# An attention and routing kernel: two pools change places, fills move ahead of a small load, token rows grow from 2052 to 2112 bytes

## Chip, core and metric

The kernel runs on one core of a Trainium2 chip. Its time is device time in microseconds of one execution; three runs of the kernel before gave 434.67, 436.81 and 437.12, median 436.81. Engines are called TensorE (PE in the rows, its weight loads PEld), VectorE (DVE), ScalarE (ACT), GpSimd (POOL) and SyncE (SP). DMA transfers are issued by SyncE's queue (SPq) and by GpSimd (POOLq) and run on the core's 16 DMA engines.

## What is computed

Attention over chunks of 32 positions, then a mixture of experts in which every token goes to exactly one of eight experts. Each expert takes at most 384 tokens, and the pairs of token and expert are served in order of their logits.

```python
for c in range(nc):                       # 24 chunks of 32, for 4 x 8 heads of 64
    k_full = np.concatenate([mem_k, k_ctx], axis=2)      # 8 memory keys, 16 left, 32, 8 right
    scores = scale * np.matmul(q_c, k_full.transpose(0, 1, 3, 2))
    a = np.exp(scores - max); a = a / (sum + 1e-09)
    out[:, :, c_start:c_end] = np.matmul(a, v_full)
x = out.transpose(0, 2, 1, 3).reshape(3072, 512)
logits = x @ w_gate                       # 3072 x 8
for idx in np.argsort(-logits.flatten()): # greedy, an expert full at 384 tokens
    ...
for e in range(8):
    out[mask] = np.maximum(x[mask] @ w1[e], 0.0) @ w2[e] # 512 -> 1024 -> 512
```

## The kernel before

**Attention.** The 3072 tokens are 24 tiles of 128. `attention` runs them as a software pipeline written out by hand: `plan` lists its steps (scores, softmax, transposes, product with the values, norm, rows, logits) with the number of tiles by which each lags. Keys and values come in through five buffers `kvb` in the pool `kvbuf`, which are filled with zeros once at the start by VectorE, ScalarE and GpSimd. Right after these fills GpSimd makes the identity matrix for the transposes (L75, L76). All other tiles of the attention are in the pool `abuf`.

**Token rows.** `rows` writes each attention row as a pair of half-precision parts into the tile `keep` (L173, L174), 24 rows of `XW` elements a partition. `release` adds the scale of the row, one 32-bit number in the last two elements (L181), and writes the 128 rows of a tile to the DRAM tensor `xs` (L182). Tiles 0 to 20 are released late, when the last keys and values have been asked for: ten of them in one go by `rest`, near 107 us. The last two, 22 and 23, wait for the last norms, between the steps of the first routing. One such transfer is 128 pieces of `XW` elements.

**Routing.** `phase` finds the tokens of an expert by a histogram search on VectorE and TensorE and ends in a number of an expert, `ei` (L551). Small transposes of an identity on TensorE (`fill`, L466) fill its idle time in the first phase. `tokens` makes the list `ids` (L653) and gathers the expert's 384 rows from `xs` into three tiles `xg` by indirect DMA from GpSimd (L658). For the first expert three things stand ahead of the gathers on GpSimd: `farr`, an indirect gather of 128 times the same row of the constants, that nothing reads; `seen`, a load of four bytes from each 128th row of `xs`, that nothing reads either, but that makes GpSimd wait for all writes of `xs`; and fills of one partition of each `xg`.

**Experts.** `loads` brings the weights `w1f`, `w2f` from SyncE, four transfers of half a megabyte for each matrix, at an address that SyncE loads from `ei` (L748, L751). `weights` takes the largest value (L770 on ScalarE; for the first expert half of the last part on VectorE, L773), makes a power of two of it, and rounds the weights to a high part (ScalarE) and a low one (GpSimd). `turn` transposes the first expert's rows on TensorE (L688); later ones are transposed by DMA (L670). `gemm` multiplies: L902 and L912 into `ps_hid`, L929 into `ps_y`. `output` scales the result by the number that came along in the row (L878) and `scatter` writes it out.

**What sets the order.** From the routing on, `Lines` merges these generators by costs and due times when the kernel is built; each engine then runs its instructions in that order, and the framework adds the semaphore waits. Pools are stacks of tiles in the on-chip memory. `abuf` was opened first and `kvbuf` after it; both close when the attention is done, and `wbuf`, which holds `xg`, the weights and all else of the experts, begins at the place where the first of them began. A transfer into `wbuf` therefore waits for those that used that place.

Of the kernel before, what the change touches and what calls it, by code (L numbers as in the profile page):

```python
# [11 lines left out]
F32 = mybir.dt.float32  # L12
F16 = mybir.dt.float16
BF16 = mybir.dt.bfloat16
I32 = mybir.dt.int32
AF = mybir.ActivationFunctionType
ALU = mybir.AluOpType
AX = mybir.AxisListType

P = 128  # L20
# [5 lines left out]
DM = H * D  # L26
# [2 lines left out]
NG = CAP // P  # L29
KC = DM // P  # L30
FC = FF // P
XW = 2 * DM + 2
WF = 16
BIG = float(1 << 23)

# [19 lines left out]
def attention(g):  # L55

    nc, ab, pp = g.nc, g.abuf, g.psum
# [10 lines left out]
    for i in range(1, NB):  # L68
        for r, e in ((slice(0, L.q), i), (slice(L.k1, L.end), i + 1)):
            if e % 3 == 1:  # L70
                nc.scalar.activation(kvb[i][:, r], g.zero.to_broadcast([P, L.q]), AF.Copy)
            else:
                (nc.vector if e % 3 == 0 else nc.gpsimd).memset(kvb[i][:, r], 0.0)
    keep = ab.tile([P, NT, XW], F16, name="keep")
    make_identity(nc, g.ident)  # L75
    nc.gpsimd.tensor_copy(g.ident16, g.ident)  # L76
    st = {}
# [100 lines left out]
    def release(_, i=None):  # L178
        if i is None:
            i = st["next"] = st.get("next", -1) + 1  # L180
        nc.scalar.activation(keep[:, i, 2 * DM:XW].bitcast(F32), st[i]["pr"][:, 1], AF.Copy)  # L181
        nc.sync.dma_start(g.xs[i * P:(i + 1) * P, :], keep[:, i])  # L182

    def rest(_):
# [60 lines left out]
    for t in range(n):  # L245
        for f, d in plan:
            i = t - d
# [376 lines left out]
def tokens(g, k, out, lo, hi, e):  # L624

    nc, v, rb = g.nc, g.nc.vector, g.rbuf
    soon = 5.0 if k < 2 else 0.4
    xg = out["xg"] = [g.wbuf.tile([P, XW], F16, tag="xg", name="xg", bufs=3 * NG) for _ in range(NG)]
    if k == 0:
        yield POOL, 3.0, 0.0  # L630
        far = rb.tile([P, 1], I32, tag="far", name="far", bufs=1)
        nc.gpsimd.memset(far, 0)
        nc.gpsimd.indirect_dma_start(out=rb.tile([P, g.consts.shape[1]], F32, tag="farr", name="farr", bufs=1), out_offset=None, in_=g.consts,
                                     in_offset=bass.IndirectOffsetOnAxis(ap=far, axis=0))
        seen = rb.tile([1, NT, 2], F16, tag="seen", name="seen", bufs=1)
        nc.gpsimd.dma_start(seen, g.xs.rearrange("(t p) c -> p t c", p=P)[0:1, :, 0:2])
        for x in xg:
            nc.gpsimd.memset(x[0:1], 0.0)
    p = yield PE, 0.45 if k < 1 else 0.27, e + (ROOM if k else SEM), soon
    pair = g.D[:, 108:204]  # L640
    for j in range(0, NT, 4):
        nc.tensor.matmul(pair, lo[:, j // 4].rearrange("p x v c -> p (x v c)"), hi[:, :, j:j + 4], start=(j == 0), stop=(j + 4 == NT))
    e = yield DVE, 0.25, p + LATE, soon
    own = rb.tile([P, NT, 4], BF16, tag="own", name="own", bufs=1)
    v.tensor_tensor(own, pair.rearrange("p (u c) -> p u c", c=4), g.own.unsqueeze(1).to_broadcast([P, NT, 4]), op=ALU.mult)
    p = yield PE, 0.06, e + SEM, soon
    nc.tensor.matmul(pair, g.put, own.rearrange("p u c -> p (u c)"), start=True, stop=True)
    e = yield DVE, 0.5, p + LATE, soon
    idf = rb.tile([P, NG, 8, 4], F32, tag="idf", name="idf", bufs=1)
    ids = rb.tile([P, NG], I32, tag="ids", name="ids", bufs=3)  # L650
    v.tensor_tensor(idf, pair.rearrange("p (a w c) -> p a w c", a=NG, w=8),
                    g.row.unsqueeze(1).unsqueeze(3).to_broadcast([P, NG, 8, 4]), op=ALU.mult)
    v.tensor_reduce(ids, idf.rearrange("p a w c -> p a (w c)"), axis=AX.X, op=ALU.max)  # L653
    out["ids"] = ids
    at = out["at"]
    for a in range(NG):
        t = yield POOL, 1.27, e + SEM, soon
        d = nc.gpsimd.indirect_dma_start(out=xg[a], out_offset=None, in_=g.xs,  # L658
                                     in_offset=bass.IndirectOffsetOnAxis(ap=ids[:, a:a + 1], axis=0))
        at.append(max(t, g.lines.clk[DMA]) + (2.5 if k == 0 else 3.0))  # L660
        g.held.append((at[-1], d))

    yield NONE, 0.0, out["xfree"]
    x = g.wbuf.tile([P, 2 * KC, CAP], F16, tag="x2", name="x2", bufs=2)
    out.update(xh=x[:, 0:KC], xl=x[:, KC:])
    for a in range(NG):
        s = slice(a * P, (a + 1) * P)
        if k:
            t = yield TURN, 1.8, lambda: at[a]
            d = nc.sync.dma_start_transpose(x[:, :, s], xg[a][:, 0:2 * DM])  # L670
            t += 3.2
            g.turned.append((t, d))
            continue
        g.lines.add(turn(g, out, a, x[:, :, s], soon), soon)
    if k:
        out["x"] = t + SEM
# [26 lines left out]
def pow2(g, rb, src, shape, top, name, bufs=2):  # L703


    out = {}
    finish(pow2_steps(g, rb, src, shape, top, name, bufs, out))
    return out["pr"]
# [49 lines left out]
def weights(g, k, st, n):  # L758

    nc, v, rb = g.nc, g.nc.vector, g.rbuf  # L760
    fl = st["f" + n]
    due = -1000.0 * (2 * k + int(n))
    first = k == 0 and n == "1"
    m = 5 if first else 4
    am = rb.tile([P, 6], F32, tag="am" + n, name="am" + n, bufs=1)
    for j in range(4):
        w = 512 if first and j == 3 else 1024
        t = yield ACT, 0.25 + w / 1024, lambda: fl[j][1] if len(fl) > j else INF, due
        jk = g.wbuf.tile([P, 1024], F16, tag="jk16", name="jk16", bufs=1)
        nc.scalar.activation(jk[:, 0:w], fl[j][0][:, 0:w], AF.Abs, accum_out=am[:, j:j + 1])  # L770
    if first:
        u = yield DVE, 0.75, lambda: fl[3][1], 7.0
        v.tensor_reduce(am[:, 4:5], fl[3][0][:, 512:], axis=AX.X, op=ALU.max, apply_absolute_value=True)  # L773
        t = max(t, u)
    soon = 0.0 if k else 6.0
    t = yield DVE, 0.15, t + SEM, soon
    v.tensor_reduce(am[:, 5:6], am[:, 0:m], axis=AX.X, op=ALU.max if n == "1" else ALU.add)
    t = yield PE, 0.12, t + SEM, soon
    nc.tensor.transpose(g.D[0:1, 256:256 + P], am[:, 5:6], g.ident)
    t = yield DVE, 0.75, t + LATE, soon  # L780
    name, top = "s" + n, 7 if n == "1" else 14
    m = rb.tile([1, 1], F32, tag=name + "m", name=name + "m", bufs=1)
    v.tensor_reduce(m, g.D[0:1, 256:256 + P], axis=AX.X, op=ALU.max)
    pr = pow2(g, rb, m, [1, 1], top, name, bufs=1)
    t = yield PE, 0.1, t + SEM, soon
    halves = pr.rearrange("p a b -> p (a b)").bitcast(BF16).rearrange("p (a t) -> p a t", t=2)
    nc.tensor.matmul(g.D[:, 106:108], g.one_row, halves[:, :, 1], start=True, stop=True)
    if n == "1":
        st["s1t"] = t
    t = yield ACT, 0.17, t + LATE, soon  # L790
    s = rb.tile([P, 2], F32, tag=name + "s", name=name + "s", bufs=3)
    nc.scalar.activation(s, g.D[:, 106:108], AF.Copy)
    st["s" + n] = s
    t = max(t, (yield NONE, 0.0, st["free" + n]))
    h, l = (g.wbuf.tile([P, 4, 1024], F16, tag=f"w{n}{x}", name=f"w{n}{x}", bufs=2) for x in "hl")
    st["w" + n] = h, l
    if n == "2":
        g.lines.add(inverse(g, st, t + SEM), 0.5)
    if k == 0:
        g.lines.add(rounded(g, st, n, h, l, s, t + SEM, fl))  # L800
        return
    for j in range(4):
        f, _, used = fl[j]
        t = yield ACT, 1.1, t, due
        nc.scalar.activation(f, f, AF.Copy, scale=s[:, 0:1])  # L805
        t = yield ACT, 1.06, t, due
        nc.scalar.activation(h[:, j], f, AF.Copy)  # L807
        st["h" + n][2 * j] = st["h" + n][2 * j + 1] = t + SEM
        g.lines.add(low(g, st, n, j, slice(0, 1024), l[:, j], f, h[:, j], t + SEM, 1.0, used), 0.0)
# [65 lines left out]
def output(g, k, st, a, py, t, bank):  # L875
    t = yield DVE, 0.8, t
    y = g.wbuf.tile([P, DM], F32, tag="y", name="y", bufs=3)
    g.nc.vector.tensor_scalar(y, py, st["inv"], st["xg"][a][:, 2 * DM:XW].bitcast(F32), op0=ALU.mult, op1=ALU.mult)  # L878
    g.lines.bank[bank].append(t + SEM)
    t = yield POOL, 1.1, t + SEM  # L880
    scatter(g, y, st["ids"][:, a:a + 1])
    if a == NG - 1:
        st["out"] = t
# [139 lines left out]
def attention_moe(ctx: ExitStack, tc: tile.TileContext, kv, w_gate, w1, w2, consts, out):  # L1023
    nc = tc.nc
    g = Ctx()
    g.nc, g.tc, g.kv, g.w1, g.w2, g.out = nc, tc, kv, w1, w2, out
    g.scat, g.consts = [], consts
    g.SIGN = -2147483648
    g.xs = tc.dram_tile([N, XW], F16, name="xs")
    g.fixed = ctx.enter_context(tc.tile_pool(name="fixed", bufs=1))  # L1030
# [12 lines left out]
    g.D = lasting.tile([P, 512], F32, name="D")  # L1043
    st = [{} for _ in range(E)]
    with tc.manual_schedule():
        with (tc.tile_pool(name="abuf", bufs=1) as g.abuf, tc.tile_pool(name="kvbuf", bufs=1) as g.kvbuf,
              tc.tile_pool(name="psum_a", bufs=1, space=bass.MemoryType.PSUM) as psum):
            g.psum = Banks((psum, dict(A=2, B=2, C=1)))
            g.lines, g.cold, g.open, g.filler = Lines(g), INF, False, None
# [125 lines left out]
```

## Time and profile before

| | |
|---|---|
| median of three runs | 436.81 us |
| the profiled execution | 433.79 us, of it 432.0 us span |
| busy in the span | PE 385.0 us (89%), ACT 310.2, DVE 287.0, POOL 261.3 |
| written to DRAM and read from it | 12.60 MB, 69.33 MB |
| share of the chain of waits | PE 65%, DMA 12%, DVE 8% |

The durations below are from the profiled execution, and a change of so many microseconds there is taken over to the median. The attention goes to about 108 us, the first routing from there to 129, the first expert's matmuls start at 140.75, and the eighth's results leave at the end. TensorE's high share is an average: between the two halves it has little to do but `fill`.

### The profile page before, as it was taken

Reading aid. Unit: us, or ns where it says so; the run is one execution under the profiler, and the core shown is the slowest. Engines: PE = TensorE matmul, PEld = TensorE weight load, DVE = VectorE, ACT = ScalarE, POOL = GpSimd, SP = SyncE. Lnnn points to the kernel's source line nnn. Section 1 sums busy time; section 2 is a strip of 40 time slices with the busy share of each in tenths; the row PEclk is TensorE's granted clock in tenths of the full one; section 3 lists DMA queues with packets and bytes.
Section 4 is the critical chain, followed back from the end, with each engine's and each line's share of the span. In section 5 each row is a group of like instructions: output and inputs, shape, how many; then the busy total and the mean of one; then the engine's idle time right before and its main releaser. Section 6 shows DMA issues by size and latency. Waiting matters only on the chain.

```text
span 432.0 us, 10842 instructions
## 1 busy us (share of the span) xinstructions
PE 385.0 (89%) x4098; PEld 236.3 (55%) x4098; DVE 287.0 (66%) x1101; ACT 310.2 (72%) x513; POOL 261.3 (60%) x225
## 2 busy tenths in 40 slices
PE   1879998987674999699999999999999999999993
PEld 1667777765563654345456456546545545545541
DVE  5466786987885778848868877868877863222310
ACT  6277887886205876949868986996887999997800
POOL 6056665654235978847485585675648748947721
PEclk9999999999998899989999999999999999999997
DMA  6899998965987409915943971990792598931001
GB/s 235 359 348 315 355 325 294 357 218 199 213 134 282 174 2 340 221 49 197 327 85 99 364 126 40 338 233 24 228 320 64 170 347 245 341 69 49 2 24 49
DMA packets 43139, 88.12 MB, mean 204 GB/s; under 512 B 25232, under 2 KB 25360, under 8 KB 40144
## 3 DMA queue, kind: packets, MB, share of 16 engines
q1 hardware_dynamic: 38848, 73.88, 55.2%
q0 software_dynamic: 3952, 13.05, 8.5%
q8 instruction: 32, 0.52, 0.5%
q10 hardware_dynamic: 288, 0.51, 0.3%
q14 instruction: 19, 0.16, 0.1%
HBM read 69.33 MB, written 12.60 MB: 190 GB/s over the span
## 4 chain that ended last, share of the span: by engine, by line
PE 65%; DMA 12%; DVE 8%; issue 5%; ACT 3%; POOL 2%; SPq 2%; POOLq 0%; DVEq 0%; ACTq 0%
PE ps_hid L912 25%; PE ps_y L929 22%; DMA kvb<-in_kv_dram 7%; PE ps_av L138 4%; DMA w1f<-in_w_dram 3%; PE ps_s L104 3%; PE ps_pt L123 2%; PE D L402 2%; PE D L203 1%; DMA xg<-xs,ids 1%; PE ps_xt L192 1%; DMA x<-xg 1%; POOL w2l L852 1%; SPq L670 1%; PE ps_hid L902 1%
## 5 line engine op out<-in xcount | busy, mean ns | idle before, releaser
L912 PE MATMUL ps_hid<-x,w1h 128*128 128x384 f16 x496 | 95.4, 329 | 2.3 <-DMA x<-xg 2.3
L852 POOL TENSOR_TENSOR w2l<-w2f,w2h 128x1024 f16<-128x1024 f32 x32 | 68.0, 2131 | 35.4 <-ACT w2h L807 35.3
L852 POOL TENSOR_TENSOR w1l<-w1f,w1h 128x1024 f16<-128x1024 f32 (+1 forms) x33 | 68.1, 2073 | 19.0 <-ACT w1h L807 18.2
L912 PEld LDWEIGHTS <-w1h 128*128 128x128 f16 x496 | 46.6, 98 | 32.0 <-ACT jk L770 2.4
L929 PEld LDWEIGHTS <-hh 128*128 128x128 f16 x384 | 35.6, 98 | 37.0 <-issue 0.2
L912 PE MATMUL ps_hid<-x,w1l 128*128 128x384 f16 x256 | 53.5, 327 | 0.0
L870 DVE SCALAR_TENSOR_TENSOR hl<-ps_hid,hh 128x384 f16<-128x384 f32 x64 | 35.3, 552 | 22.0 <-ACT hh L867 22.0
L867 ACT ACTIVATE hh<-ps_hid 128x384 f16<-128x384 f32 x64 | 31.0, 484 | 25.4 <-PE ps_hid L912 25.1
L929 PE MATMUL ps_y<-w2h,hh 128*128 128x512 f16 x192 | 48.2, 379 | 0.0
L929 PE MATMUL ps_y<-w2l,hh 128*128 128x512 f16 x192 | 48.1, 379 | 0.0
L770 ACT ACTIVATE jk<-w1f 128x1024 f16<-128x1024 f32 (+1 forms) x32 | 33.3, 1041 | 20.5 <-DMA w1f<-in_w_dram 19.8
L929 PE MATMUL ps_y<-w2h,hl 128*128 128x512 f16 x192 | 46.5, 379 | 0.0
L172 POOL TENSOR_TENSOR xr<-x,sxp 128x512 f32<-128x512 f32 x24 | 25.0, 1041 | 33.0 <-DVE sxp L724 20.9
L174 POOL TENSOR_TENSOR keep<-xr,keep 128x512 f16<-128x512 f32 x24 | 27.1, 1128 | 25.0 <-ACT keep L173 24.8
L104 PE MATMUL ps_s<-kvb 128*32 128x128 f32 x768 | 29.0, 291 | 14.1 <-DMA kvb<-in_kv_dram 13.7
L878 DVE TENSOR_SCALAR y<-ps_y,inv,xg 128x512 f32<-128x512 f32 x24 | 19.4, 806 | 26.9 <-PE ps_y L929 26.2
L937 POOL DMA_INDIRECT out_dram<-y,ids x24 | 23.9, 997 | 20.8 <-DVE y L878 17.1
L770 ACT ACTIVATE jk<-w2f 128x1024 f16<-128x1024 f32 x32 | 33.7, 1053 | 2.6 <-DMA w2f<-in_w_dram 1.0
L658 POOL DMA_INDIRECT xg<-xs,ids x24 | 23.1, 962 | 17.1 <-DVE R L335 9.9
L912 PEld LDWEIGHTS <-w1l 128*128 128x128 f16 x256 | 24.6, 98 | 15.2 <-issue 0.5
L104 PEld LDWEIGHTS ps_s<-kvb 128*32 128x32 f32 x768 | 22.9, 117 | 17.6 <-issue 11.0
L805 ACT ACTIVATE w2f<-w2f,s2s 128x1024 f32<-128x1024 f32 x28 | 31.9, 1141 | 0.5
(189 smaller groups left out, 765.5 us busy)
## 6 DMA issues: line engine op xcount, KB each, us to landing
kvb<-in_kv_dram SPq DMA_DIRECT2D x46, 580.0 KB, 6.3
w1f<-in_w_dram SPq DMA_DIRECT2D x32, 512.0 KB, 5.6
w2f<-in_w_dram SPq DMA_DIRECT2D x32, 512.0 KB, 8.7
xs<-keep SPq DMA_DIRECT2D x24, 256.5 KB, 5.2
kvb<-in_kv_dram SPq DMA_DIRECT2D x2, 320.0 KB, 3.2
kvb<-in_kv_dram SPq DMA_DIRECT2D x2, 260.0 KB, 4.7
cc<-in_consts_dram ACTq DMA_DIRECT2D x1, 438.0 KB, 9.2
xg<-xs,ids POOLq DMA_INDIRECT x24, 4.8
```

Source lines behind the costliest of these rows:

```text
L104: nc.tensor.matmul(o, s["q"][:, pr, c, :], s["k"][:, :, 2 * pr + c // 2, 0:2 + c % 2:1 + c % 2], start=True, stop=True, tile_position=(0, ...
L172: nc.gpsimd.tensor_tensor(xr, s["x"], sx[:, 0].to_broadcast([P, DM]), op=ALU.mult)
L174: nc.gpsimd.tensor_tensor(row[:, DM:2 * DM], xr, row[:, 0:DM], op=ALU.subtract)
L658: d = nc.gpsimd.indirect_dma_start(out=xg[a], out_offset=None, in_=g.xs, in_offset=bass.IndirectOffsetOnAxis(ap=ids[:, a:a + 1], axis=0))
L770: nc.scalar.activation(jk[:, 0:w], fl[j][0][:, 0:w], AF.Abs, accum_out=am[:, j:j + 1])
L805: nc.scalar.activation(f, f, AF.Copy, scale=s[:, 0:1])
L852: g.nc.gpsimd.tensor_tensor(l, f, h, op=ALU.subtract)
L867: g.nc.scalar.activation(hh[:, f], ph[:, 0:CAP], AF.Relu)
L870: g.nc.vector.scalar_tensor_tensor(hl[:, f], ph[:, 0:CAP], 0.0, hh[:, f], op0=ALU.max, op1=ALU.subtract)
L912: nc.tensor.matmul(ph[:, 0:CAP], w[:, f // 2, kc, (f % 2) * P:(f % 2) * P + P], st[x][:, kc, :], start=(n == 0), stop=(n == 3 * KC - 1))
L929: nc.tensor.matmul(py[a], h[:, f, a * P:(a + 1) * P], w[:, f, :], start=new, stop=(p == 2 and f == FC - 1))
L937: sc = g.nc.gpsimd.indirect_dma_start(out=g.out, in_=y, in_offset=None, out_offset=bass.IndirectOffsetOnAxis(ap=ids, axis=0))
```

## The change

The two attention pools are opened in the other order, so that `wbuf` lies over `kvbuf` first; `jk16`, a scratch tile of `weights`, goes from `wbuf` to the routing's pool. For the first expert the three fills of `xg` stand ahead of the load `seen`. `XW` is 1056 instead of 1026: rows of `keep`, `xs` and `xg` have 2112 bytes, of which the last 60 are zeros, filled once in `keep` at the start. The scale keeps its place in the row.

```diff
-XW = 2 * DM + 2
+XW = 2 * DM + 32
...
     keep = ab.tile([P, NT, XW], F16, name="keep")
+    nc.gpsimd.memset(keep[:, :, 2 * DM + 2:], 0.0)
     make_identity(nc, g.ident)
...
-        nc.scalar.activation(keep[:, i, 2 * DM:XW].bitcast(F32), st[i]["pr"][:, 1], AF.Copy)
+        nc.scalar.activation(keep[:, i, 2 * DM:2 * DM + 2].bitcast(F32), st[i]["pr"][:, 1], AF.Copy)
         nc.sync.dma_start(g.xs[i * P:(i + 1) * P, :], keep[:, i])
...
                                      in_offset=bass.IndirectOffsetOnAxis(ap=far, axis=0))
+        for x in xg:
+            nc.gpsimd.memset(x[0:1], 0.0)
         seen = rb.tile([1, NT, 2], F16, tag="seen", name="seen", bufs=1)
         nc.gpsimd.dma_start(seen, g.xs.rearrange("(t p) c -> p t c", p=P)[0:1, :, 0:2])
-        for x in xg:
-            nc.gpsimd.memset(x[0:1], 0.0)
...
-        jk = g.wbuf.tile([P, 1024], F16, tag="jk16", name="jk16", bufs=1)
+        jk = rb.tile([P, 1024], F16, tag="jk16", name="jk16", bufs=1)
...
-    g.nc.vector.tensor_scalar(y, py, st["inv"], st["xg"][a][:, 2 * DM:XW].bitcast(F32), op0=ALU.mult, op1=ALU.mult)
+    g.nc.vector.tensor_scalar(y, py, st["inv"], st["xg"][a][:, 2 * DM:2 * DM + 2].bitcast(F32), op0=ALU.mult, op1=ALU.mult)
...
-        with (tc.tile_pool(name="abuf", bufs=1) as g.abuf, tc.tile_pool(name="kvbuf", bufs=1) as g.kvbuf,
+        with (tc.tile_pool(name="kvbuf", bufs=1) as g.kvbuf, tc.tile_pool(name="abuf", bufs=1) as g.abuf,
```

GpSimd, from the end of the attention to the first gathers, in the kernel before. In the brackets stand the semaphores that an instruction waits for: DMAHW0 to 7 are the counters of the transfers that SyncE issues.

```order
78 L632 MEMSET far 128x1
79 L633 DMA farr<-in_consts_dram,far 128x876 [waits Pool_49]
80 L636 DMA seen<-xs 1x24x2 [waits DMAHW4_49,DMAHW5_49,DMAHW3_49,DMAHW6_49,DMAHW2_49,DMAHW7_49,DMAHW1_49,DMAHW0_49]
81 L638 MEMSET xg 1x1026 [waits PE_49,Activation_49]
82 L638 MEMSET xg 1x1026 x2
83 L658 DMA xg<-xs,ids 128x1026 [waits DVE_49,Pool_49]
84 L658 DMA xg<-xs,ids 128x1026 [waits Pool_49] x2
```

The same place of GpSimd in the changed kernel:

```order
79 L633 MEMSET far 128x1
80 L634 DMA farr<-in_consts_dram,far 128x876 [waits Pool_49]
81 L637 MEMSET xg 1x1056 [waits DMAHW3_49,DMAHW4_49,DMAHW2_49,DMAHW5_49,DMAHW1_49,DMAHW6_49,DMAHW0_49,DMAHW7_49,PE_49,Activation_49]
82 L637 MEMSET xg 1x1056 x2
83 L639 DMA seen<-xs 1x24x2
84 L659 DMA xg<-xs,ids 128x1056 [waits DVE_49,Pool_49]
85 L659 DMA xg<-xs,ids 128x1056 [waits Pool_49] x2
```

The wait for all eight counters went from `seen` to the first fill; `seen` itself now waits for nothing.

SyncE in the kernel before, from the last two writes of rows to the first transfers of the weights:

```order
73 L182 DMA xs<-keep 128x1026 [waits DMAHW2_49,Activation_49,Pool_49]
74 L182 DMA xs<-keep 128x1026 [waits DMAHW3_49,Activation_49,Pool_49]
75 L748 TENSOR_LOAD ei [waits DVE_49]
76 L751 ISA
77 L751 DMA w1f<-in_w_dram 128x1024 [waits DMAHW3_49,DMAHW4_49,DMAHW2_49,DMAHW5_49,DMAHW1_49,DMAHW6_49,DMAHW0_49,DMAHW7_49,DVE_49,PE_49]
```

And in the changed kernel:

```order
73 L183 DMA xs<-keep 128x1056 [waits DMAHW2_49,Activation_49,Pool_49]
74 L183 DMA xs<-keep 128x1056 [waits DMAHW3_49,Activation_49,Pool_49]
75 L749 TENSOR_LOAD ei [waits DVE_49]
76 L752 ISA
77 L752 DMA w1f<-in_w_dram 128x1024 [waits DMAHW3_49,DMAHW4_49,DMAHW2_49,DMAHW5_49,DMAHW1_49,DMAHW6_49,DMAHW0_49,DMAHW7_49,DVE_49,PE_49]
```

Here only the width of the rows differs. The other engines have the same instructions in the same order, but for the fill of `keep` on GpSimd ahead of the identity.

## Rows read from the trace of the kernel before

**Rows 1.** Chain that ended last, 100 to 186 us: start, duration (us), what.

```profile
129.73 6.25 DMA w1f<-in_w_dram
```

**Rows 2.** Waits of SyncE's queue: total us, times, longest.

```profile
SPq L751 <- DMA xs<-keep: 4.5, 1, 4.5
```

**Rows 3.** The line that issues the weights: duration min/median/max in ns, first and last start.

```profile
L751 SPq FUSED_REGOPS  x64: 42/46/56, 123.2 to 364.4; - x64
L751 SPq EVENT_SEMAPHORE  x53: 17/17/1002, 127.7 to 363.5; - x53
...
L751 SPq DMA_DIRECT2D w1f<-in_w_dram x32: 332/333/862, 128.1 to 361.3; - x32
```

**Rows 4.** The line that writes rows, likewise.

```profile
L182 SPq DMA_DIRECT2D xs<-keep x24: 319/338/1034, 90.2 to 120.0; - x24
...
DMA to landing us min/median/max: 2.6/5.2/13.5
```

**Rows 5.** Stretches: length, busy us (instructions), PEclk, DMA share, GB/s.

```profile
107.00:108.50 1.50, 1.32 (x29) 1.32 (x29) 1.26 (x8) 1.50 (x12) 0.00 (x0) 1.00 0.96 348
109.00:121.00 12.00, 7.77 (x124) 5.92 (x122) 10.07 (x50) 2.14 (x6) 5.03 (x6) 1.00 1.05 198
...
131.40:136.40 5.00, 0.00 (x0) 0.00 (x0) 1.14 (x5) 3.78 (x7) 3.27 (x4) 1.00 1.00 398
136.40:143.30 6.90, 5.86 (x48) 4.64 (x49) 5.20 (x21) 4.86 (x10) 3.33 (x4) 0.51 0.70 233
```

**Rows 6.** SyncE's DMA queue, 107 to 108.5, then 109 to 121: packets, MB, share.

```profile
q1 hardware_dynamic: 282, 0.51, 93.3%
...
q1 hardware_dynamic: 1288, 2.35, 104.1%
```

**Rows 7.** GpSimd's and SyncE's DMA queues, 122 to 127; landing of `farr`.

```profile
q0 software_dynamic: 66, 0.40, 54.2%
q1 hardware_dynamic: 172, 0.30, 40.3%
...
DMA to landing us min/median/max: 8.2/8.2/8.2
```

**Rows 8.** Timeline of VectorE: start, duration, in brackets the idle time before.

```profile
128.96 0.25 DVE L653 TENSOR_REDUCE ids<-idf 128x3 int32<-128x96 f32 x1
...
132.17 0.18 DVE L358 TENSOR_SCALAR k_c<-R 128x24 f32<-128x24 f32 x1
136.11 0.69 DVE L773 TENSOR_REDUCE am<-w1f 128x1 f32<-128x512 f32 x1 [3.76 <-DMA w1f<-in_w_dram]
```

**Rows 9.** Timeline of TensorE.

```profile
137.12 0.37 PE L779 MATMUL D<-ident,am 128*1 128x128 f32 x1 [5.80 <-DVE am L777]
...
140.75 2.08 PE L902 MATMUL ps_hid<-x,w1h 128*128 128x256 f16 x9 [0.17 <-ACT x L691]
...
143.28 0.82 PE L902 MATMUL ps_hid<-x,w1h 128*128 128x256 f16 x6
```

**Rows 10.** Timeline of GpSimd; landing of the gathers issued from 131.9 on.

```profile
119.94 0.10 POOL L632 MEMSET far<- 128x1 int32 x1
120.33 1.16 POOL L633 DMA_INDIRECT farr<-in_consts_dram,far  x1 [0.29 <-POOL far L632]
128.47 0.56 POOL L636 DMA_DIRECT2D seen<-xs  x1 [6.98 <-PE fill L466]
129.02 2.73 POOL L638 MEMSET xg<- 1x1026 f16 x3
131.92 1.02 POOL L658 DMA_INDIRECT xg<-xs,ids  x1 [0.17 <-POOL xg L638]
...
xg<-xs,ids POOLq DMA_INDIRECT x3, 4.1
```

**Rows 11.** Timeline of the start, GpSimd and TensorE.

```profile
7.61 0.29 POOL L76 CAST ident<-ident 128x128 f16<-128x128 f32 x1
...
14.44 1.12 PE L123 MATMUL ps_pt<-ident,pexp 128*128 128x128 f32 x4
```

## Prediction

> **What bounds the kernel now.** I read the chain of waits first: the reader is to see that TensorE carries most of it, but that at 128 to 136 us it leaves the engines and hangs on one transfer, the first expert's weights, `w1f` [rows 1]. Then the waits of SyncE: the issue of that transfer stood 4.5 us for the writes `xs<-keep` of the token rows [rows 2]. The rows of the issuing line say the same in clock times: SyncE had the expert's number and worked on the address at 123.2, its first semaphore passed at 127.7, the first `w1f` left at 128.1 [rows 3]. So the place to look is why the rows of `xs`, the last of which was issued at 120.0, landed only at 127.7, although the shortest landing of such a write is 2.6 us [rows 4].
>
> The stretches by engine answer that [rows 5]. From 107.0 to 108.5 the DMA engines, at 0.96 busy, move 348 GB/s; from 109 to 121, at 1.05 busy, only 198. Nearly all of that is the write of rows: 2.35 MB in 12 us, 196 GB/s, or 95 rows of 2052 bytes a microsecond [rows 6]. A row takes 16 engines x 1.05 x 12 us / 1145 rows = 176 ns of an engine there, and 16 x 0.96 x 1.5 / 249 = 93 ns before. Short bursts of writes run at nearly twice the speed of a long one. The rows left over at 122 then meet `farr`, a gather that the kernel issues at 120.33 [rows 10]: from 122 to 127 it holds 54% of the DMA engines' time and the rows get 0.30 MB through, 29 a microsecond [rows 7].
>
> What waits behind `w1f`: VectorE is through with its other work at 132.35 and stands 3.76 us until the fourth `w1f` lands [rows 8]; TensorE stands 5.80 us, and from 136.4 to 143.3 its granted clock is 0.51, that is 1.2 GHz [rows 5, 9]. The first matmul of the experts starts at 140.75 [rows 9].
>
> **The change part by part.**
>
> *Pools swapped, and `jk16` in another pool.* The later pool `wbuf` now lies over the key and value buffers first. I count nothing for it: in the built program the first `w1f` transfer, and the first fill of `xg` too, name the same eight hardware DMA queues as before and wait for the same counts on them, those of the last row writes. The swap would let both go earlier only if it took these waits away, and it doesn't; it moves addresses alone.
>
> *Fills of `xg` ahead of `seen`.* Nothing leaves: the queue wait moves from `seen` to the first fill. On GpSimd the old sequence is `seen` 0.56, fills 2.73, gather at 131.92 [rows 10]; the new one is 2.73 x 1056/1026 = 2.81, then 0.56, then some 0.3 us of standstill, as ahead of `farr` (0.29): the gather is 0.2 us later if the writes land when they do now. Behind it on GpSimd stand the other gathers and the scaling of `w1`. If the writes land early, it costs nothing: the fills then end long before `ids`, which VectorE has only at 129.21 [rows 8].
>
> *The fill of `keep`* is 720 elements a partition on GpSimd, between the fills of `kvb` and the identity. By the fills of `xg`, 1026 elements in 0.91 us each, it is 0.64 us; if each of its 24 pieces cost as much as the one-element fill `far`, 0.10 us [rows 10], it is 2.4. The identity is cast by 7.90 and first used at 14.44 [rows 11]; 6.5 us of cover hide it. Nothing.
>
> *Rows of 2112 bytes.* 3072 rows grow by 60 bytes: 0.18 MB written, and as much gathered; at 348 GB/s 0.5 us each way over the whole run, and of the first expert's three gathers 0.07 us. The new form's speed in a long burst is in no row. By bytes as now it is 196 GB/s, 93 rows a microsecond; by the rows of a short burst 348 GB/s, 165. Between these ends lies the whole prediction. Why it could change: 2052 is 32 x 64 + 4, so nearly each row ends in a block of 32 or 64 bytes in which the next row begins, and the memory is asked twice for part of a block. 2112 is 33 x 64, and no block is shared. That the shared blocks are the cost is my guess; for it speaks that reads are not slow: in the stretch that reads the weights, the engines get 398 GB/s [rows 5].
>
> The Trainium skill has a rule on this side, in "Collectives: The Full Stack", section "Rules for kernel authors": buffers aligned to 32 bytes spare the hardware a read-modify-write. It gives no price, and no run here shows it yet.
>
> How much is needed: from 109 to the last landing 1145 rows are written up to 121, 95 in the next microsecond and 0.30 MB or 144 after 122, about 1385. Without a queue the last lands at 120.0 + 2.6 = 122.6; that takes 1385 / 13.6 = 102 rows a microsecond, 215 GB/s in the new form, 7% more rows than now. The nearer row is that of the short burst: the same writes from the same buffer, only with no queue behind them. At 165 rows a microsecond the writes are up with ScalarE and GpSimd, and even a third of the way from 93 to 165 is enough; I take them as done at 122.6.
>
> Then SyncE goes on at 123.2, plus the 0.4 us that it now takes from the first semaphore to the first issue: `w1f` leaves at 123.6, 4.5 us earlier, and the fourth lands at about 131.5 (now 129.73 + 6.25 = 135.98 [rows 1]). Late next is VectorE: it has k=1's keys to do until 132.35, so `am` starts at 132.4 instead of 136.11: 3.7 us. The gathers keep up: they start at 129.3 instead of 131.92, the third 2.6 us behind the first as now, and lands 4.1 us later [rows 10], at 136.0; with its transposes the first expert matmul can start at 137.0, 3.75 us earlier. TensorE's idle time shrinks from 5.8 to 2.1 us, so the clock may not fall. It would give back at most about 1.2 us: nine matmuls of 256 columns take 2.08 us at the low clock, at the six in 0.82 us that follow it 1.23 [rows 9], and about as much less again on the small ones. Some of it runs into ScalarE's roundings; I take 0.4, between 0 and 1.2. Whatever comes later (GpSimd's rounding, the phases on VectorE, the matmuls) stands in order behind these instructions and moves with them.
>
> Sum: 3.7 + 0.4 = 4.1 us. The profiled execution took 433.79 us (span 432.0 and 1.79 around it), so 429.7; the median of the runs, 436.81, is 3.0 above that execution, and I take the 4.1 off the median: **432.7 us**. On its own this case goes from 430.8 (1.2 for the clock, another 1 for the scatter of runs, of which one was 434.67) to 434.4.
>
> **The rivals.**
>
> *The write limit doesn't care for the form of a row.* For it: short bursts of the same unaligned rows run at 348 GB/s, so the slow stretch may be what the memory takes in for long, with a buffer ahead of it. Against it: reads get twice that. At 196 GB/s 93 rows instead of 95 a microsecond leave 13 x 2.6 = 34 more rows at 122, and in the tail 29 go through in a microsecond: 1.2 us more, none if rows and not bytes are counted, and 0.2 for the gathers. 436.8 to 438.2, in the middle 437.5.
>
> The Trainium skill speaks for this rival in "DMA: Bandwidth & Descriptors". Its section "Latency and other measured facts" calls 207 to 214 GB/s per direction full for copies between HBM tensors, near the 196 here; and its section "How a descriptor splits into AXI transactions" starts each one at a multiple of 256 bytes, by which a row of 2052 needs nine wherever it starts, and one of 2112 at 0, 64, 128 or 192 also nine. By these rules the time would be the same, 437.5. No row here shows a long burst of aligned writes.
>
> *The tail grows*, on the other side: the writes fall behind `farr`. Each row that is still to be written at 122 costs 1/29 us there. Should the longer rows go slower per byte than now, then from 192 GB/s down (91 rows a microsecond, 55 more rows left, 1.9 us and 0.3 for the gathers) the loss passes 0.5%; at 185 GB/s it is 101 rows, 3.5 + 0.3 us, 440.6. For it: `farr` takes 8.2 us to land [rows 7] and the margin is only 2%. Against it: nothing in longer aligned rows is harder to write.
>
> **How the numbers follow.** Forecast 0.55; write limit 0.33; tail grows 0.12. Differences under 0.5%, 2.2 us, are about what a measurement of this kernel can't tell from none. So faster 0.55, same 0.33, slower 0.12. The range goes over the first and the write limit's case with its dearest end: 430.8 to 438.2; outside lie most of the 0.12 and some 0.06 below. The forecast's own range is 430.8 to 434.4.
>
> **What would show it.** Right: from 109 to 121 the rows at 215 GB/s or more, or the stretch ending early; SyncE's wait for `xs` on the first `w1f` gone; first `w1f` near 123.6; `am` near 132.4; first expert matmul near 137; the first gather near 129.3, waiting for `ids`; granted clock 1.00 there. Wrong: the DMA rate at 190 to 200 GB/s from 109 on and `w1f` again at 128; or the writes early and yet the matmul at 140, with a wait on another engine; or the 4 us given back at a later expert.

## The result, and the profile after

The changed kernel took **430.0 us** (median of 20 runs, 425.64 to 436.69), the kernel before, run 17 more times beside it, 435.03 (median of 20, 431.29 to 437.68). The ratio is 0.987, 95% interval 0.985 to 0.990. The forecast, 432.7 us, was right in direction and too high in value: 430.0 lies 0.8 below its range. The profiled execution took 428.82 us, span 427.0; that of before 433.79 and 432.0. So 5.0 us are to be placed. Ratios and their intervals, here and below, leave out the runs that lie more than 1.5% above the fastest of the same kernel; the medians do not.

Stretches of the changed kernel, same columns as [rows 5]; the last is the new low stretch of the clock:

```profile
107.00:108.50 1.50, 1.50 (x32) 1.50 (x29) 1.29 (x8) 1.47 (x10) 0.00 (x0) 1.00 0.97 353
109.00:121.00 12.00, 7.81 (x122) 6.06 (x123) 9.97 (x48) 1.63 (x4) 5.58 (x6) 1.00 0.61 226
131.40:136.40 5.00, 1.99 (x22) 1.48 (x23) 4.13 (x17) 2.46 (x6) 2.16 (x3) 0.95 0.50 151
135.93:139.34 3.41, 3.29 (x28) 2.77 (x29) 2.20 (x8) 3.16 (x6) 3.10 (x4) 0.50 0.71 190
```

SyncE's DMA queue from 109 to 121, then GpSimd's and SyncE's from 122 to 127, as in [rows 6, 7]:

```profile
q1 hardware_dynamic: 1430, 2.68, 60.2%
...
q1 hardware_dynamic: 220, 0.84, 55.5%
q0 software_dynamic: 70, 0.38, 23.9%
```

From 109 to 121 more bytes than before go through (2.68 MB against 2.35) in 0.60 of the engines' time instead of 1.04. Bytes by busy time, 2.68 MB / (12 us x 0.602), are 371 GB/s; before it was 2.35 / (12 x 1.041) = 188. By 115 the queue is worked off; in the six us behind that the engines are busy for 0.24 of the time, so no queue is left for `farr` to meet, and the share of GpSimd's DMA queue from 122 to 127 falls from 54.2% to 23.9%. The changed kernel, columns as above:

```profile
109.00:115.00 6.00, 3.92 (x60) 3.09 (x61) 4.83 (x27) 0.81 (x2) 1.16 (x2) 1.00 0.98 361
115.00:121.00 6.00, 3.89 (x66) 2.97 (x63) 5.15 (x22) 0.81 (x2) 4.42 (x5) 1.00 0.24 90
```

The lines that write rows and issue weights, as in [rows 3, 4], each one line lower in the code:

```profile
L183 SPq DMA_DIRECT2D xs<-keep x24: 319/370/1012, 89.4 to 119.5; - x24
...
L752 SPq EVENT_SEMAPHORE  x53: 2/17/1032, 122.7 to 360.7; - x53
...
L752 SPq DMA_DIRECT2D w1f<-in_w_dram x32: 258/333/1868, 123.1 to 358.7; - x32
```

The first `w1f` leaves at 123.1, 3.5 us after the last write of rows was issued (119.5); before it was 128.1 and 120.0. The wait of [rows 2] is in the list of waits no more.

GpSimd, as in [rows 10]:

```profile
119.85 1.16 POOL L634 DMA_INDIRECT farr<-in_consts_dram,far  x1 [0.29 <-POOL far L633]
122.10 2.81 POOL L637 MEMSET xg<- 1x1056 f16 x3 [1.09 <-PE D L542]
124.86 0.56 POOL L639 DMA_DIRECT2D seen<-xs  x1
129.47 1.02 POOL L659 DMA_INDIRECT xg<-xs,ids  x1 [4.04 <-DVE R L336]
```

VectorE and TensorE, as in [rows 8, 9]:

```profile
128.42 0.25 DVE L654 TENSOR_REDUCE ids<-idf 128x3 int32<-128x96 f32 x1
...
131.62 0.18 DVE L359 TENSOR_SCALAR k_c<-R 128x24 f32<-128x24 f32 x1
132.10 0.69 DVE L774 TENSOR_REDUCE am<-w1f 128x1 f32<-128x512 f32 x1 [0.29 <-ACT jk L771]
```

```profile
133.10 0.27 PE L780 MATMUL D<-ident,am 128*1 128x128 f32 x1 [2.34 <-DVE am L778]
...
136.05 1.01 PE L689 MATMUL ps_xg<-ident,xg 128*128 128x128 f16 x8 [0.96 <-DMA xg<-xs,ids]
136.85 2.13 PE L903 MATMUL ps_hid<-x,w1h 128*128 128x256 f16 x9
```

The chain of waits there now goes over the gathers and no more over `w1f` [rows 1]:

```profile
129.47 0.72 POOL xg L659
130.19 0.60 issue
130.79 0.96 POOL xg L659
131.75 0.30 issue
132.05 3.86 DMA xg<-xs,ids
135.91 0.14 issue
136.05 1.01 PE ps_xg L689 x8
137.06 1.92 PE ps_hid L903 x9
```

**Where the 5.0 us are.** I take the start of the same instruction in both traces. `ids` is 0.54 us earlier (128.42 against 128.96 [rows 8]); the first expert matmul 3.90 (136.85 against 140.75 [rows 9]); the second expert's first 4.52; the end of the span 4.93. So 0.54 came before the point where the change bears, 3.36 between `ids` and the first expert matmul, 0.62 up to the second expert and 0.41 behind it. The 0.62 is TensorE's wait at the second expert, 2.35 us before and 1.71 after (before first, then after):

```profile
184.59 2.72 PE L912 MATMUL ps_hid<-x,w1h 128*128 128x384 f16 x8 [2.35 <-DMA x<-xg]
```

```profile
180.07 2.53 PE L913 MATMUL ps_hid<-x,w1h 128*128 128x384 f16 x8 [1.71 <-ACT jk L771]
```

At the last 0.41 the kernel before waited 0.58 us for the largest value of a later `w1f`, and the one after didn't:

```profile
315.92 0.27 PE L779 MATMUL D<-ident,am 128*1 128x128 f32 x1 [0.58 <-DVE am L777]
```

### The profile page after: what moved, and what is told of

Its sections match the earlier page's. It is cut to its first block, busy times and chain, and to the rows that moved or that the text cites. A ratio compares the mean times of both kernels' runs of the same rounds, so it can differ in the third digit from the quotient of the medians.

```text
span 427.0 us, 10843 instructions
## 1 busy us (share of the span) xinstructions
PE 384.0 (90%) x4098; PEld 235.4 (55%) x4098; DVE 286.6 (67%) x1101; ACT 310.2 (73%) x513; POOL 263.0 (62%) x226
## 4 chain that ended last, share of the span: by engine, by line
PE 68%; DMA 9%; DVE 8%; issue 5%; ACT 5%; POOL 3%; SPq 0%; POOLq 0%; DVEq 0%; ACTq 0%
PE ps_hid L913 27%; PE ps_y L930 25%; DMA kvb<-in_kv_dram 8%; PE ps_av L139 3%; PE ps_s L105 3%; PE D L403 2%; PE ps_pt L124 2%; PE D L204 1%; PE ps_xt L193 1%; ACT w1f L806 1%; POOL w2l L853 1%; DMA xg<-xs,ids 1%; PE ps_hid L903 1%; PE D L532 1%; DVE x L154 1%
## 5 line engine op out<-in xcount | busy, mean ns | idle before, releaser
L175 POOL TENSOR_TENSOR keep<-xr,keep 128x512 f16<-128x512 f32 x24 | 28.0, 1166 | 23.4 <-ACT keep L174 23.1
L806 ACT ACTIVATE w1f<-w1f,s1s 128x1024 f32<-128x1024 f32 x28 | 31.8, 1137 | 0.6
```

The lines of the kernel that those rows point to most:

```text
L175: nc.gpsimd.tensor_tensor(row[:, DM:2 * DM], xr, row[:, 0:DM], op=ALU.subtract)
```

## Experiments

Each run's medians stand beside those of the kernel before on the same chip. Two places of each trace are compared: from the issue of the last write of rows to the first `w1f`, and from `ids` to the first expert matmul. "GB/s busy" is SyncE's DMA queue from 112 to 121 us: MB by 9 us and its share.

| kernel | row, bytes | GB/s busy | last row to `w1f`, us | `ids` to matmul, us |
|---|---|---|---|---|
| before | 2052 | 186 | 8.05 | 11.79 |
| before, once more (e11) | 2052 | 184 | 8.50 | 12.17 |
| rest only (e2) | 2052 | 187 | 6.60 | 10.75 |
| aligned `keep` (e7) | 2052 | 175 | 10.86 | 15.48 |
| changed kernel | 2112 | 372 | 3.54 | 8.43 |
| changed, again (e5) | 2112 | 371 | 3.56 | 9.27 |
| rows only (e1) | 2112 | 378 | 3.54 | 9.05 |
| without `farr` (e4; e6) | 2112 | 374; 376 | 3.54; 3.55 | 8.39; 8.37 |
| 2052 of each 2112 written (e8) | 2052 | 360 | 3.55 | 8.42 |
| written from byte 4 on (e13) | 2108 | 371 | 3.54 | 8.39 |
| width (e3) | 2080 | 368 | 3.54 | 9.46 |
| width (e9) | 2064 | 366 | 3.55 | 8.88 |
| width (e14) | 2056 | 317 | 3.55 | 8.61 |
| width (e10) | 2116 | 295 | 3.61 | 9.08 |
| width (e15) | 2068 | 248 | 3.61 | 8.81 |
| halves (e12; e16) | 2052; 2112 | 365; 370 | 5.57; 5.32 | 14.98; 14.66 |

**Which part of the change.** The kernel before with the new rows alone:

```diff
-XW = 2 * DM + 2
+XW = 2 * DM + 32
...
+    nc.gpsimd.memset(keep[:, :, 2 * DM + 2:], 0.0)
...
```

> The kernel before with the rows of 2112 bytes alone (pools, fills and jk16 as before). Theory, the rows are all of it: 430.0 us, ratio to before 0.987, the same as the full change within 0.5 us; last write of rows lands near 121.5, first w1f issued at 123.1 (128.08 before), first expert matmul near 137. Rival, the swap of the pools gives part of it (in the profile 0.55 us of the 5.0 are there before 108 us, in the attention): 430.6 to 431, and the rows begin to be written at 90.2 as before. Rival, the fills matter: with seen ahead of the fills the first gather would leave later than 129.5; since the writes land at 121.5 I expect no difference there.

And the other half, the pools, `jk16` and the fills, with `XW = 2 * DM + 2`:

> The change without its rows: rows of 2052 bytes, pools swapped, jk16 moved, fills ahead of seen. Theory, the rows are all of it: 435.0 us, ratio 1.000 (0.998 to 1.003), up to 0.2 us slower for the fills; w1f at 128.1; rows from 109 to 121 at 196 GB/s. Rival, the swap gives the 0.55 us of the attention: 434.4, ratio 0.9987, and the first write of rows issued near 89.4 and not 90.2.

Rows alone: median 429.6 (12 runs) against 432.64 (35 runs), 3.0 lower. The rest: 432.51, 0.1 lower. On this chip the runs of before lay anywhere from 427.1 to 439.2, and the ratio makes less of the first: 0.999 (0.995 to 1.003), and 1.006 (1.002 to 1.010) for the rest; the 0.987 that was expected for the rows alone was not met. By times alone the share of the rows is not proven; by stages it is. SyncE's wait for the rows is gone with the rows alone and stands with the rest alone (e2):

```profile
SPq L751 <- DMA xs<-keep: 3.0, 1, 3.0
```

The first row's write was issued at 89.4 and 89.9. In the four profiles with the old order of the pools it was between 89.4 and 93.1, in the twelve with the new order that left the attention alone between 89.2 and 91.8: the 0.54 us ahead of `ids` lie within this scatter, and no gain from the pools is to be seen. The fills cost nothing to be seen.

**The gather that nothing reads.**

```diff
-        far = rb.tile([P, 1], I32, tag="far", name="far", bufs=1)
-        nc.gpsimd.memset(far, 0)
-        nc.gpsimd.indirect_dma_start(out=rb.tile([P, g.consts.shape[1]], F32, tag="farr", name="farr", bufs=1), out_offset=None, in_=g.consts,
-                                     in_offset=bass.IndirectOffsetOnAxis(ap=far, axis=0))
```

> The changed kernel without far and farr, the gather of constants that nothing reads. Theory, with the fast rows nothing is late behind it: 430.0 us within 0.5 us, first gather at 129.5 waiting for ids. Rival, farr pays for something at the first gather on GpSimd: then the first real gathers land later than 3.9 us after their issue and the first expert matmul is later by as much, 431 to 433 us. Rival, farr still takes DMA time from the last rows: w1f before 122.5, and up to 0.5 us gained.

> The changed kernel without far and farr, beside the full change on one chip. Its median was 428.5 on the chip where rows alone gave 429.6. Theory, farr costs and saves nothing now: the same median as the full change within 0.7 us. Rival, it still costs: 1 us or more below the full change.

428.53 (12 runs) on the chip of e1, and on another 430.48 (8 runs) beside the full change:

> The full change once more, on the chip of this call. Its rows alone gave a median 3.0 us below before's on another chip (12 and 35 runs, before between 427.1 and 439.2), the full change 5.0 on the first one (20 and 20 runs). Theory, the gain is about 4 us everywhere and the rest is scatter of runs of about 1%: 3 to 5 us below before's median, ratio 0.988 to 0.993. Rival, the pools and fills add 1 to 2 us to what the rows give: 5 us or more below again.

430.87 (6 runs) against 434.49 for before (13 runs), 3.6 lower; ratio 0.990 (0.984 to 0.995), without `farr` 0.989 (0.985 to 0.993). The medians without and with `farr` differ by 0.4 us, which 8 and 6 runs can't tell from nothing: a cost or a gain of `farr` is not shown.

**What makes the rows slow.** First the two ends apart: rows back to back in DRAM from an aligned `keep`, and rows of 2052 bytes at a pitch of 2112.

```diff
-    g.xs = tc.dram_tile([N, XW], F16, name="xs")
+    g.xs = tc.dram_tile([N, 2 * DM + 2], F16, name="xs")
...
-        nc.sync.dma_start(g.xs[i * P:(i + 1) * P, :], keep[:, i])
+        nc.sync.dma_start(g.xs[i * P:(i + 1) * P, :], keep[:, i, 0:2 * DM + 2])
...
```

> The changed kernel with keep still 1056 elements a row, so that each row starts at a multiple of 64 bytes on the chip, but rows of 2052 bytes back to back in DRAM. Theory, the blocks in DRAM: slow as before, mean of a row's packet 150 to 200 ns from 111 us on, 85 to 110 rows a microsecond, w1f issued 6.5 us or more after the last write of rows (8.05 before, 3.54 with 2112 or 2080 bytes). Rival, the source's start counts: 90 ns a packet and 3.5 us.

```diff
-        nc.sync.dma_start(g.xs[i * P:(i + 1) * P, :], keep[:, i])
+        nc.sync.dma_start(g.xs[i * P:(i + 1) * P, 0:2 * DM + 2], keep[:, i, 0:2 * DM + 2])
...
```

> The changed kernel, but of each row only the first 2052 bytes are written, to rows that start every 2112 bytes in DRAM; the 60 bytes left are zeroed by a transfer of their own early in the attention (its time and the attention's are not to be compared). Each row then ends inside a block, but no block holds parts of two rows. Theory, two rows in one block is the cost: fast, 90 ns a packet, w1f 3.5 us after the last write of rows. Rival, a part of a block is the cost, whoever else writes there: slow, 150 ns or more, since each row still has one such part; between the two if the cost goes by parts, of which a row has two with 2052 back to back.

SyncE's queue from 109 to 121, first e7, then e8:

```profile
q1 hardware_dynamic: 1141, 2.08, 106.2%
```

```profile
q1 hardware_dynamic: 1610, 2.95, 67.8%
```

e7 is slow, e8 fast: the same 2052 bytes cost less than half as much engine time (by MB and share, 163 and 363 GB/s) when no two rows meet in a block. In e8 the attention ends some 7 us later, but the rate holds over the whole long burst there: from 114 to 124 it is 3.13 MB at 86.8%, 361 GB/s. An aligned source did not help, and a part of a block at a row's end costs nothing by itself. Nor does one at its start:

> The changed kernel, pitch 2112, but each row is written from its fifth byte on (2108 bytes); the four bytes ahead are zeroed by a transfer of their own early in the attention (its time and the attention's are not to be compared). No two rows share a block, but each row starts 4 bytes into one. Theory, two rows in one block: fast, 90 ns a packet from 109 us on. Rival, a start that is no multiple of 16 bytes: slow, 120 ns or more, 150 to 200 if it is all of it.

371 GB/s. So neither an unaligned start nor an unaligned end is enough; what e7 has and these two haven't is a neighbour in the same block, and with it a pitch that is no multiple of 16 bytes. Rows with gaps between them at such a pitch, which would tell these two apart, were not run. What alignment is needed, the widths tell (`XW` alone changed):

> The changed kernel with rows of 2080 bytes, 65 x 32 and 32.5 x 64. Theory, blocks of 32 bytes: no block of 32 is shared, so as fast as with 2112: 430.0 us, rows from 109 on at 350 GB/s or more, w1f at 123. Theory, blocks of 64 bytes: half of the row borders lie inside a block, so about half of the loss: rows near 250 GB/s. At 215 GB/s and more the writes still keep up, so the time would be 430 to 431 by that too; the rate tells them apart. Rival, only the even multiple of 64 counts: 435 us, 196 GB/s.

> The changed kernel with rows of 2064 bytes, 129 x 16 and 64.5 x 32. Theory, blocks of 32 bytes: every second border between rows lies inside a block, so about half of the stalls of 2052: mean of a row's packet 120 to 150 ns from 109 to 121 us, 115 to 140 rows a microsecond, w1f 3.5 to 5 us after the last write of rows. Theory, blocks of 16 bytes or less: 90 ns, 175 rows a microsecond, 3.54 us.

> The changed kernel with rows of 2056 bytes, 257 x 8. Rows of 2064 (129 x 16) were fast. Theory, blocks of 16 bytes: half of the row borders lie inside one, so stalls about half as many as with 2052: 120 to 150 ns a packet from 109 to 121 us, w1f 4 us or more after the last write of rows. Rival, blocks of 8 or 4 bytes or an odd multiple of 4: 90 ns, 3.5 us.

> The changed kernel with rows of 2116 bytes, 66 x 32 + 4: longer than 2112, and again with two rows in one block at nearly each border. Theory, shared blocks: slow as with 2052, mean of a packet 150 to 210 ns from 109 to 121 us, w1f 6.5 us or more after the last write of rows, first expert matmul 140 or later, 433 to 436 us. Rival, a length over 2100 bytes or the other pools are what helped: 90 ns, 3.54 us, 430 us.

> The changed kernel with rows of 2068 bytes, 129 x 16 + 4. Starts and shared blocks are of the same kind as with 2052 and 2116 (4 bytes further in each row). Theory, shared blocks or starts alone: like 2052, 150 to 200 ns a packet from 111 us on. Rival, the nearness of the pitch to 2048 adds to it, neighbouring rows then being written to the same place modulo 2048: between 2052 and 2116, nearer to 2052, 130 to 180 ns; if the length alone decided, as much as 2064, 90 ns.

Rows that begin at multiples of 32 or 16 bytes run at full speed, which contradicts my blocks of 32 and 64. At multiples of 8 (2056) there are some stalls, at odd multiples of 4 more. By MB and share, as in the table, a row of 2056 bytes took 104 ns of an engine, one of 2116 took 115, of 2068 133 and of 2052 176. For 2056 I had expected 120 ns or more and `w1f` after 4 us or more, for 2116 and 2068 150 ns or more. The theory missed all three; only the rival's range for 2068, 130 to 180 ns, holds what was measured. 2116 and 2068 share as many blocks as 2052 and stall less: something besides sharing, perhaps the pitch, is left open. Nearness to 2048, that rival, does not explain it by itself, since 2056 and 2064 are nearer and faster. For the kernel it doesn't matter: with whole tiles of any of these widths but 2052 the queue was gone in time and `w1f` left within 3.61 us of the last row. The total times of these runs say less: 429.69 us for 2080 (12 runs), and in single runs 427.95 for 2064, 427.76 for 2056, 431.38 for 2068 and 436.0 for 2116; 434.34 for e7. Single runs of the kernel before beside them gave 430.39 (2064, 2116) and 436.62 (2056, 2068). With 2116 the seventh expert's first matmul came 21.22 us after the sixth's first `ps_y`, in before 16.94 us; 2.21 us of that TensorE waited for ScalarE. Why it did is open, so 2116 is not shown to pay in total time. The single runs of e8 (434.89), e13 (437.68), e12 (434.57) and e16 (432.89) were made of more transfers and are not to be compared.

Last the order: even rows of a tile, then odd ones, so that neighbours never follow each other within a transfer.

```diff
-        nc.sync.dma_start(g.xs[i * P:(i + 1) * P, :], keep[:, i])
+        for o in range(2):
+            nc.sync.dma_start(g.xs[i * P + o:(i + 1) * P:2, :], keep[o:P:2, i])
```

> The kernel before (2052 bytes), but each tile's rows are written by two transfers, even rows and then odd rows, 64 each, so that rows next to each other in DRAM never follow each other within a transfer. Theory, a stall comes when two writes to one block are close together in one transfer's order: fast or nearly so, 90 to 120 ns a packet. Rival, any two writes to the block, whatever their order, cost: slow as before, 150 to 210 ns from 109 to 121 us. SyncE issues 48 transfers in place of 24, some 3 us more in the run of ten tiles at 107, so the total time is not to be compared.

> The changed kernel (2112 bytes) with even and odd rows of a tile written by two transfers of 64 rows. With 2052 bytes in this form packets took 86 ns, but only 99 rows a microsecond got through with the engines half busy. Theory, halves of 64 rows keep only half of the engines busy, whatever the row's form: the same 95 to 110 rows a microsecond and 86 ns here, so the speed there was not set by stalls. Rival, the 99 rows a microsecond of 2052 are the stalls in another shape: then 150 rows or more here.

From 109 to 121, 2052 bytes and then 2112:

```profile
q1 hardware_dynamic: 1347, 2.21, 50.2%
```

```profile
q1 hardware_dynamic: 1402, 2.36, 53.0%
```

Both forms ran alike, at half of the engines' time. The limit was the issuing: SyncE was held 0.594 us (median) by each half in e12, against 0.338 us by a whole tile in before [rows 4], and the halves landed 2.5 us (median) after their issue, so no queue built up.

```profile
L183 SPq DMA_DIRECT2D xs<-keep x48: 451/594/1790, 91.3 to 125.9; - x48
...
DMA to landing us min/median/max: 2.0/2.5/6.7
```

From 115.65 to 121.46 nine halves were issued one right behind the other, one each 0.65 us: 64 rows in 0.65 us are some 99 a microsecond, the rate that went through. With 2052 bytes the stalls were gone. Whether by the order or by the lower rate these runs don't tell. The kernel before, once more, showed how its own stage scatters:

> The kernel before, for the scatter of its own stages on another chip. Theory: slow rows again, but how late the last one lands varies, so the first w1f 6 to 11 us after the last write of rows (8.05 and, with the other pools, 6.60 and 10.86 so far), always over the 3.54 us of the aligned rows; 432 to 437 us.

It took 432.1 us; the first `w1f` left 8.50 us after the last write of rows, within what was expected.

## Why the forecast was right, and where it was wrong

**Right: the mechanism.** The writes went far beyond the 215 GB/s needed; the wait of SyncE is gone; `w1f` left at 123.1 (said: 123.6), `am` started at 132.10 (132.4), the first gather at 129.47 (129.3), the first expert matmul at 136.85 (137.0). The swap, the fills and the fill of `keep` did nothing that these runs show. Both rivals fell: the speed of the writes does depend on the form of a row, and the tail shrank.

**Wrong: the base and the room left for it.** The step that failed is "I take the 4.1 off the median", with "another 1 for the scatter of runs". The 436.81 was the median of three runs; of 20 it is 435.03, 1.78 lower, and that is two thirds of the miss of 2.7 us. Single runs of before have a standard deviation of 1.8 us on that chip, so the median of three is uncertain by about 1.2 (the spread of the medians of all threes of the 20 runs); the profiled execution, 3.0 us below the median, was itself a run of this kernel and a warning that was read and not used. From 435.03 the same sum gives 430.9, inside the range. (The low end of the range, by its own terms 436.81 - 3.7 - 1.2 - 1, is 430.9 too, not 430.8.) The other third, 0.9 us, is the gain: 5.0 by the medians and not 4.1. That is within the scatter: single runs of the changed kernel have a standard deviation of 2.8 us, so the median of 20 is uncertain by some 0.8 (an estimate from that spread).

**The sum.** On three chips the medians differ by 5.0, 3.0 (rows alone) and 3.6 us; 4.1 lies among them. Inside the pair of profiles the terms were not what I wrote, though, and that they add up so near is in part luck. (a) The stage of [rows 8, 9], said to give 3.75, gave 3.36 from `ids` to the matmul; the clock times agree only because `ids` was 0.54 us early. From `ids` to the first `ps_y` it is 32.61 us in before and 32.03 in e11, 29.26 after and 29.14 in e5: 2.8 to 3.5 us for the whole stage, against 4.1 said, the clock included. (b) The gather was put right behind `ids`, at 129.3 for an `ids` that is ready at 129.21. It left 0.80 us after the end of `ids` (129.47 - 128.67), and 0.80 to 0.88 in every other profile in which the rows were early: a mis-sized 0.7 us on what is now the chain. It is no price of every gather: those of the second to the seventh expert left 0.27 to 0.28 us after the end of their `ids` (the second's at 166.13, with `ids` from 165.61 to 165.86). The first one also waits for GpSimd's own counter (line 84 of its order), as `farr` does, which stood 0.29 us; what makes up the rest is not shown. (c) The clock, 0.4 us: nothing. It still fell, at 135.93, after TensorE had stood 2.34 us and was standing again, for 3.41 us instead of 6.8 (granted clock 0.50, that is 1.2 GHz); but from the first expert matmul to the first `ps_y` it is 20.83 us, and was 20.82 before (136.85 to 157.68, 140.75 to 161.57). In other profiles this span is 19.86 (e11) and 20.08 (e2) with the old rows, 19.87 (e5) and 20.03 (e1) with the new: nothing of it goes with the rows. The "granted clock 1.00 there" was wrong. (d) Nothing was counted for the 0.54 in the attention and the 1.03 behind the first expert. Both are scatter: the wait at the second expert was 2.35 in before, 1.71, 2.17 (e5) and 2.03 (e1) with the new rows, and 0.18 us in e2 and 0.59 in e11, which have the old ones.

**The guess about shared blocks** was right in kind as far as e7, e8 and e13 go (an unaligned start or end without a neighbour cost nothing) and wrong in size: borders at multiples of 16 bytes cost nothing. That sharing is all of it is not shown, and 2068 and 2116 speak against it. The Trainium skill's rule in "Collectives: The Full Stack", section "Rules for kernel authors", that buffers aligned to 32 bytes spare a read-modify-write, agrees in direction; here unaligned starts and ends without a neighbour were free, and 16 were enough. Two places of the Trainium skill stood on the other side, both in "DMA: Bandwidth & Descriptors". The 207 to 214 GB/s of its section "Latency and other measured facts" are said of copies between HBM tensors; taking them for a limit of these writes was a misreading, for rows of 2112 were written from on-chip memory at 371 GB/s. And by the section "How a descriptor splits into AXI transactions" of the same page of the Trainium skill a row of 2052 and one of 2112 come to nine transactions each (an estimate), while the engine time of a row differs by nearly a factor of two here (175 and 91 ns): that count does not tell what these writes cost.

## What to carry to other kernels

Where rows of some 2 KB are written back to back to DRAM in a long burst, try a pitch of a multiple of 16 bytes (2064, 2080 and 2112 were fast here; with only part of each row written, 2112 was). The sign to look for is a DMA share above 0.95 with GB/s at half of what another stretch reaches. Before a wait is priced, look up how long the next one behind it takes from producer to consumer in the same trace; the new chain here was the gathers, and their start was 0.7 us later than I had counted. And a forecast is as uncertain as its base: three runs of a kernel that scatters by 1.8 us fix it to no better than 1.2.

## What was not expected of the hardware

- A write of 2052 bytes with neighbours held a DMA engine nearly twice as long under load (16 x 12 us x 1.041 / 1145 rows = 175 ns, from 109 to 121) as one of 2112 (16 x 12 x 0.602 / 1269 = 91 ns). Rows of 2064 and 2080 bytes, which start at multiples of 16, were as fast as 2112 (366 and 368 GB/s against 372).
- A transfer of 64 rows from every second partition held SyncE longer at its issue than one of 128 rows from all of them (median 0.594 us in e12 and e16 and 0.338 in before, shortest 0.451 and 0.319), so that the DMA engines were only half busy (0.50 and 0.53), whatever the row. Why the issue takes longer is not shown.
- The first gather on GpSimd started 0.80 us after the end of the VectorE instruction that makes its indices, those of the second to the seventh expert 0.27 to 0.28 us after theirs.
